# Block products for w_down, and one written list of steps: a transformer layer with linear attention and a bilinear GLU

## The chip, the cores and the metric

The kernel runs on one core of a Trainium2 chip. The metric is the device time of one execution in microseconds (us). Times before are the median of three runs; the profile is of one further execution. A core has TensorE (PE: matmuls, with PEld for weight loads), VectorE (DVE), ScalarE (ACT), GpSimd (POOL) and SyncE (SP), which here only issues transfers. Each works through its own queue in order.

## The reference

```python
xn = layernorm(x)                                  # x: 2048 tokens x 512, bf16
q, k, v = split(xn @ wqkv)                         # 32 heads of 16
phi(t) = concat(softmax(t @ w_phi), softmax(-(t @ w_phi)))   # 32 features a head
kv, z  = sum over tokens of phi(k) v and of phi(k)
attn   = (phi(q) kv) / (phi(q) z + 1e-6) @ wo
glu    = ((xn @ w_gate) * (xn @ w_up)) @ w_down    # hidden width 1792
out    = x + attn + glu
```

## The kernel before

The 2048 tokens are 16 tiles of 128; four tiles make a group (T is 0 to 3). The hidden width is 14 chunks of 128 columns. `wgu` holds w_gate and w_up, `wd` w_down, `wo` the output weights, all in SBUF for the whole run. The program is scheduled by hand: each engine runs its instructions in the order in which the Python code issues them.

1. Start (to about 12 us): the first four tiles are centred and transposed on TensorE, and v is computed for them.
2. Groups 0 and 1, with the k side: `half` makes a gate or an up chunk for 512 tokens with four matmuls of 512 columns, `gate_copy` takes the gate to SBUF on ScalarE, `hidden` multiplies on VectorE into `hT`. In between come `fold` (w_phi folded into the k and q weights), v and k of each tile, and `features`: two exponentials on ScalarE, a reduction (L300) and a reciprocal (L302) on VectorE, and the feature product on GpSimd (L304). `kv` sums phi(k) v into two PSUM tiles. The load of the transposed q weights is issued on SP (L659) behind the first four transposes of normalized tiles and ahead of the next eight.
3. `attend(n)` divides and makes `otok`, which SP's queue transposes to `oT`. `fin(n)` is one output tile: 14 matmuls of `hT` with `wd` and 4 of `oT` with `wo`, all into one bank of 512 columns; VectorE adds x, and SP sends the tile out (L387, L398, L399).
4. Groups 2 and 3: gate and up are computed by seven block products instead of eight. `pair_block(k, g)` takes 1024 tokens as two row blocks, the 512 inputs as two inner blocks, and the chunks k and k + 7 as two column blocks. It needs sums of tokens (`ss`, L454), sums of weights (`T`, L445, four for each k, half of them on VectorE), and products p1 to p7 that ScalarE keeps (L493, L495) and VectorE joins (L499, L503). For the up half, GpSimd multiplies by the gate (L504). Output tiles 4 to 7 fill the gaps between the products.
5. From about 181 us: output tiles 9 to 15, with the last q tiles and `attend` one tile ahead. The last tile is cut at 384 columns, so that the last bank has 128 columns.

w_gate and w_up are scaled by powers of two, one for each pair of chunks (`weight_norm`, `weight_up`). PSUM is eight banks: six in rotation (`bank`) and two for the pool of the phase (v, kv, attention, or `fin`).

Of the kernel before, what the change touches and what calls it, by code (L numbers as in the profile page):

```python
# [15 lines left out]
PSUM = bass.MemoryType.PSUM  # L16


def _bcast_ap(ap_in: bass.AP, new_ap):
    return bass.AP(tensor=ap_in.tensor, offset=ap_in.offset, ap=new_ap)  # L20


@with_exitstack
def kernel(
# [40 lines left out]
    consts = ctx.enter_context(tc.tile_pool(name="consts", bufs=1))  # L65
    wpool = ctx.enter_context(tc.tile_pool(name="wpool", bufs=1))
# [7 lines left out]
    wgu = wpool.tile([P, 2, DC, F], BF16)  # L74
# [60 lines left out]
    xnT = xpool.tile([P, DC, HALF], BF16)  # L135
# [11 lines left out]
    for i in range(NV):  # L147
        vt = vpool.tile([P, 8, 4, E1], BF16, name=f"vt{i}", tag="vt")
        nc.vector.memset(vt[:, :, :, DH:E1], 1.0)
        vts.append(vt)  # L150
# [9 lines left out]
    def bank(name, dt=F32, n=TT):  # L160
        return ps_s.tile([P, n], dt, name=name, tag="s")
# [26 lines left out]
    def subtract(n, *means):  # L188
        xns[n] = xnpool.tile([P, D], BF16, name="xn", tag="x")
# [12 lines left out]
    def centre_by_halves(n):  # L202
        h = D // 2
        part = consts.tile([P, 2], F32)
        junk = xnpool.tile([P, 2, h], BF16, name="junk", tag="x")
# [5 lines left out]

    chores = []

    def chore(k=1):
        for _ in range(min(k, len(chores))):
            chores.pop(0)()

    def ln_block(lo):
        mv = mv_tile()
        nb = lnpool.tile([P, GT], F32, name="nb", bufs=GT)  # L220
        rstd = []

        def scales():
            r = lnpool.tile([P, GT], F32, name="rstd", bufs=GT)
            ln_rstd(mv, GT, r[:])
            nm = lnpool.tile([P, GT], F32, name="nm")
            nc.gpsimd.tensor_scalar(out=nm[:], in0=mv[:, :, 0], scalar1=-1.0, scalar2=None, op0=ALU.mult)
            nc.gpsimd.tensor_tensor(out=nb[:], in0=nm[:], in1=r[:], op=ALU.mult)
            rstd.append(r)

        def apply(i):
            late = lo + i >= QT
            xn = xnpool.tile([P, D], F16 if late else BF16, name="xn", tag="x")
            if late:
                nc.gpsimd.tensor_scalar(out=xn[:], in0=xall[:, lo + i, :], scalar1=rstd[0][:, i:i + 1],
                                        scalar2=nb[:, i:i + 1], op0=ALU.mult, op1=ALU.add)
            else:
                nc.scalar.activation(out=xn[:], in_=xall[:, lo + i, :], func=AF.Identity,
                                     scale=rstd[0][:, i:i + 1], bias=nb[:, i:i + 1])
            nc.sync.dma_start(out=xt(lo + i), in_=xn[:], transpose=True)  # L240

        for i in range(GT):
            chores.append(lambda i=i: ln_stats(lo + i, mv[:, i, :]))
        chores.append(scales)
        for i in range(GT):
            chores.append(lambda i=i: apply(i))
# [18 lines left out]
    def fold(qk, dst, j0):  # L265
        R = P // 2
        banks = [bank("pq").rearrange("p (j c x) -> p j c x", j=2, c=DC) for r in range(2)]
        for j in range(2):
            for c in range(DC):
                for r in range(2):  # L270
                    rows = slice(r * R, (r + 1) * R)
                    nc.tensor.matmul(banks[r][:, j, c, :], lhsT=wT2[rows, qk, c, (j0 + j) * P:(j0 + j + 1) * P],  # L272
                                     rhs=bd[rows, c, 4 * r:4 * r + 4, :].rearrange("p a b -> p (a b)"),
                                     start=True, stop=True)
        dv = dst[:, j0:j0 + 2, :].rearrange("p j (c r x) -> p r j c x", c=DC, r=2)
        nc.scalar.copy(out=dv[:, 0], in_=banks[0])
        nc.vector.tensor_copy(out=dv[:, 1], in_=banks[1])

    def fold_both(qk, dst):
        for j0 in (0, 2):  # L280
            fold(qk, dst, j0)
# [6 lines left out]
    def features(n, w, name, pf=None):  # L288
        if pf is None:
            pf = bank(name)  # L290
            proj(pf, n, w)
        e = epool.tile([P, NG, 2, 4 * DH], F32, name="e")
        pfv = pf.rearrange("p (g c) -> p g c", g=NG)
        nc.scalar.activation(out=e[:, :, 0, :], in_=pfv, func=AF.Exp,  # L294
                             scale=rst[:, n:n + 1] if n < GT else 1.0)
        nc.scalar.activation(out=e[:, :, 1, :], in_=pfv, func=AF.Exp,  # L296
                             scale=nrst[:, n:n + 1] if n < GT else -1.0)
        ev = e[:].rearrange("p g s (h f) -> p (g s h) f", f=DH)
        sums = epool.tile([P, 2 * H], F32, name="sums")
        nc.vector.tensor_reduce(out=sums[:], in_=ev, axis=AX.X, op=ALU.add)  # L300
        rs = epool.tile([P, 2 * H, 1], F32, name="rs")
        nc.vector.reciprocal(out=rs[:].rearrange("p a b -> p (a b)"), in_=sums[:])  # L302
        phi = epool.tile([P, NG, P], BF16, name=f"phi{name}", tag="phi", bufs=4)
        nc.gpsimd.tensor_tensor(out=phi[:].rearrange("p g (x f) -> p (g x) f", f=DH), in0=ev,  # L304
                                in1=rs[:].to_broadcast((P, 2 * H, DH)), op=ALU.mult)
        return phi

    sends = []

    def qproj(n, held=False, new_bank=bank):  # L310
        q_begin(n, new_bank)
        q_end(held)

    q_open = []

    def q_begin(n, new_bank):
        pf = new_bank("q")
        proj(pf, n, W1q, lower)
        q_open.append((n, pf))

    def q_end(held=False):
        q_rest()
        q_features(held)

    def q_rest():
        n, pf = q_open[0]
        proj(pf, n, W1q, upper)

    def q_features(held=False):
        n, pf = q_open.pop()  # L330
        phiq = features(n, W1q, "q", pf)

        def send():
            phiqTs[n] = qtpool.tile([P, NG, P], BF16, name="phiqT")
            nc.sync.dma_start(out=phiqTs[n][:], in_=phiq[:].rearrange("p g c -> p (g c)"), transpose=True)

        sends.append(send)
        if not held:
            qsend()

    def qsend():
        sends.pop(0)()

    hTs = {}
    units = [(T, f) for T in range(NGRP // 2) for f in range(FC)]
# [8 lines left out]
    def gate_copy(ps, n):  # L354
        g_sb = gpool.tile([P, TT], BF16, name="g_sb")
        nc.scalar.copy(out=g_sb[:, 0:n], in_=ps)  # L356
        return g_sb

    def hidden(T, f, ps, g_sb, lo, hi):
        if T not in hTs:  # L360
            hTs[T] = hpool.tile([P, FC, TT], BF16, name="hT", tag="h")
        nc.vector.tensor_tensor(out=hTs[T][:, f, lo:hi], in0=ps, in1=g_sb[:, 0:hi - lo], op=ALU.mult)  # L362

    def unit(T, f, lo=0, hi=TT):
        pg = half(wg, "g", T, f, lo, hi)
        pu = half(wu, "u", T, f, lo, hi)
        hidden(T, f, pu, gate_copy(pg, hi - lo), lo, hi)

    def ffn(k):
        for _ in range(k):  # L370
            if units:
                unit(*units.pop(0))

    def fin_parts(n, new_bank, lo=0, hi=D):
        T, t4 = n // GT, n % GT
        w = hi - lo
        held = []

        rows = [(hTs[T][:, f, t4 * P:(t4 + 1) * P], wd[:, f, lo:lo + w]) for f in range(FC)]
        rows += [(oTs[n][:, c, :], wo[:, c, lo:lo + w]) for c in range(DC)]  # L380
        if n == 2 * GT:
            rows = [row for f, row in enumerate(rows) if f % FH != FH - 1 or f >= FC] + [rows[FH - 1], rows[FC - 1]]

        def mm(i):
            if i == 0:
                held.append(new_bank("fin")[:, 0:w])
            nc.tensor.matmul(held[0], lhsT=rows[i][0], rhs=rows[i][1], start=(i == 0), stop=(i == len(rows) - 1))  # L387
            if i == len(rows) - 1:
                store(held[0])

        def store(ps):
            o_sb = opool.tile([P, w], BF16, name=f"o_sb{w}", bufs=3 if w == D else 1)
# [10 lines left out]
    def fin(n, cuts=(0, D)):  # L403
        for lo, hi in zip(cuts, cuts[1:]):
            for part in fin_parts(n, bank, lo, hi):
                part()
# [374 lines left out]
    with tc.tile_pool(name="ps_ab2", bufs=1, space=PSUM) as ps_ab:  # L781
# [11 lines left out]
        for n in range(9, NT):  # L793
# [5 lines left out]
            if sends:  # L799
                qsend()  # L800
# [33 lines left out]
```

## Time and profile before

| | |
|---|---|
| median of three runs | 215.61 us (215.32 to 215.88) |
| the profiled execution | 215.67 us, span 213.9 us |
| granted TensorE clock | 1.00 |
| busy, share of the span | TensorE 98%, weight loads 48%, VectorE 76%, ScalarE 58%, GpSimd 60% |

The span runs from the first to the last instruction; the profiled execution's own time holds 1.8 us more. Matmuls are pipelined, so a row's mean duration of 379 ns is not what a matmul costs in a stream: their starts are. The same holds on the other engines to a smaller degree.

### The profile page before, as it was taken

The numbers are of one execution on the slowest core, as the hardware profiler recorded it, in microseconds if no ns is written. First come the engines' busy times: TensorE is split into PE (matmuls) and PEld (weight loads), VectorE is DVE, ScalarE is ACT, GpSimd is POOL, SyncE is SP. The second block draws the span as 40 slices with busy tenths as digits, with TensorE's granted clock in tenths as the row PEclk, the third lists the DMA queues.
The fourth block names the chain that finished last, engine by engine and source line by source line (L and its number), as shares of the span: only waits on it lengthen the run. The fifth ranks groups of instructions, "written<-read, shape, count | busy, mean of one in ns | idle before, by whom it ended". The sixth has DMA issues, their size and how long they took to land.

```text
span 213.9 us, 3610 instructions
## 1 busy us (share of the span) xinstructions
PE 210.1 (98%) x1280; PEld 101.7 (48%) x1280; DVE 163.2 (76%) x279; ACT 125.0 (58%) x219; POOL 129.2 (60%) x112
## 2 busy tenths in 40 slices
PE   8999999999999999999999999999999999999994
PEld 3664445444444444554444444444444444444543
DVE  5757979869867788887777897988969689776341
ACT  4635578998896999442666686868746352220000
POOL 3600557597895788859899497979788620333000
PEclk9999999999999999999999999999999999999999
DMA  5999995613022023234444202021120201333511
GB/s 152 266 281 385 374 287 87 91 26 75 0 51 52 0 49 81 66 40 112 100 101 100 49 0 52 0 74 25 48 49 3 74 26 34 91 98 98 126 49 49
DMA packets 47249, 19.91 MB, mean 93 GB/s; under 512 B 37504, under 2 KB 46976, under 8 KB 47104
## 3 DMA queue, kind: packets, MB, share of 16 engines
q1 hardware_dynamic: 47232, 19.69, 36.6%
q8 instruction: 10, 0.16, 0.3%
q14 instruction: 7, 0.06, 0.1%
HBM read 8.67 MB, written 2.10 MB: 50 GB/s over the span
## 4 chain that ended last, share of the span: by engine, by line
PE 98%; ACT 1%; DVE 0%; issue 0%
PE fin L387 29%; PE g L350 11%; PE u L350 11%; PE sa L487 11%; PE pv L285 7%; PE q L285 6%; PE k L285 6%; PE sc L487 6%; PE sb L487 3%; PE kv L622 2%; PE ab L686 2%; PE warm L554 2%; PE pq L272 1%; PE tp L253 1%; ACT k L493 0%; ACT xnT L256 0%
## 5 line engine op out<-in xcount | busy, mean ns | idle before, releaser
L387 PE MATMUL fin<-wd,hT 128*128 128x512 bf16 (+2 forms) x238 | 54.1, 366 | 0.0
L304 POOL TENSOR_TENSOR phiq<-e,rs 128x1024 bf16<-128x1024 f32 x16 | 30.9, 1934 | 25.6 <-DVE rs L302 18.1
L304 POOL TENSOR_TENSOR phik<-e,rs 128x1024 bf16<-128x1024 f32 x16 | 30.9, 1933 | 24.2 <-DVE rs L302 17.3
L300 DVE TENSOR_REDUCE sums<-e 128x64 f32<-128x1024 f32 x32 | 38.7, 1208 | 9.0 <-ACT e L296 9.0
L350 PEld LDWEIGHTS <-wgu 128*128 128x128 bf16 x240 | 23.1, 98 | 24.2
L387 PEld LDWEIGHTS <-hT 128*128 128x128 bf16 x238 | 22.3, 98 | 24.4
L350 PE MATMUL u<-xnT,wgu 128*128 128x512 bf16 (+1 forms) x120 | 29.1, 365 | 0.0
L350 PE MATMUL g<-xnT,wgu 128*128 128x512 bf16 (+1 forms) x120 | 28.9, 365 | 0.0
L504 POOL TENSOR_TENSOR hT<-u_sb,hT 128x512 bf16<-128x512 bf16 x18 | 21.1, 1185 | 10.1 <-DVE u_sb L503 10.1
L362 DVE TENSOR_TENSOR hT<-u,g_sb 128x512 bf16<-128x512 f32 (+1 forms) x30 | 18.6, 622 | 4.5 <-PE u L350 3.9
L356 ACT CAST g_sb<-g 128x512 bf16<-128x512 f32 (+1 forms) x30 | 17.1, 569 | 8.1 <-PE g L350 7.9
L294 ACT ACTIVATE e<-q 128x512 f32<-128x512 f32 x12 | 7.2, 598 | 23.6 <-PE q L285 23.6
L302 DVE RECIPROCAL rs<-sums 128x64 f32<-128x64 f32 x32 | 17.7, 552 | 2.5
L493 ACT ACTIVATE k<-sa,both 128x512 f32<-128x512 f32 x21 | 14.5, 688 | 8.7 <-PE sa L487 8.6
L495 ACT COPY k<-sa 128x512 f32<-128x512 f32 x21 | 12.3, 587 | 11.2 <-DVE u_sb L503 7.4
L398 DVE TENSOR_TENSOR o_sb<-fin,xall 128x512 bf16<-128x512 f32 (+2 forms) x13 | 8.4, 646 | 12.0 <-PE fin L387 12.0
L445 POOL TENSOR_TENSOR T<-wgu,T 128x512 f16<-128x512 bf16 x14 | 17.0, 1216 | 0.5
L387 PE MATMUL fin<-wo,oT 128*128 128x512 bf16 (+2 forms) x68 | 17.1, 366 | 0.0
L487 PEld LDWEIGHTS <-T 128*128 128x128 f16 x112 | 10.8, 98 | 13.1 <-issue 0.6
L487 PE MATMUL sa<-ss,T 128*128 128x512 f16 x56 | 16.7, 379 | 0.1
L435 ACT ACTIVATE wgu<-wgu,up 128x1024 bf16<-128x1024 bf16 x14 | 15.9, 1156 | 0.1
L420 ACT ACTIVATE junk<-wgu 128x1024 bf16<-128x1024 bf16 x14 | 15.1, 1083 | 0.0
(98 smaller groups left out, 352.1 us busy)
## 6 DMA issues: line engine op xcount, KB each, us to landing
out_dram<-o_sb SPq DMA_DIRECT2D x15, 128.0 KB, 1.9
wd<-in_B_w_down_dram SPq DMA_DIRECT2D x1, 1792.0 KB, 15.4
wgu<-in_B_w_gate_dram SPq DMA_DIRECT2D x2, 640.0 KB, 6.8
wgu<-in_B_w_up_dram SPq DMA_DIRECT2D x2, 640.0 KB, 8.0
xall<-in_A_x_dram SPq DMA_DIRECT2D x1, 1024.0 KB, 12.1
xall<-in_A_x_dram SPq DMA_DIRECT2D x4, 128.0 KB, 2.7
vk<-in_A_wqkv_dram SPq DMA_DIRECT2D x2, 256.0 KB, 3.6
wgu<-in_B_w_gate_dram SPq DMA_DIRECT2D x2, 256.0 KB, 4.9
```

The costliest lines, as they stand in the source:

```text
L285: nc.tensor.matmul(ps, lhsT=xt(n)[:, j, :], rhs=w[:, j, :], start=(j == 0), stop=(j == DC - 1))
L300: nc.vector.tensor_reduce(out=sums[:], in_=ev, axis=AX.X, op=ALU.add)
L302: nc.vector.reciprocal(out=rs[:].rearrange("p a b -> p (a b)"), in_=sums[:])
L304: nc.gpsimd.tensor_tensor(out=phi[:].rearrange("p g (x f) -> p (g x) f", f=DH), in0=ev, in1=rs[:].to_broadcast((P, 2 * H, DH)), op=ALU.mult)
L350: nc.tensor.matmul(ps, lhsT=w[:, c, f * P:(f + 1) * P], rhs=xnT[:, c, T * TT + lo:T * TT + hi], start=(c == 0), stop=(c == DC - 1))
L356: nc.scalar.copy(out=g_sb[:, 0:n], in_=ps)
L362: nc.vector.tensor_tensor(out=hTs[T][:, f, lo:hi], in0=ps, in1=g_sb[:, 0:hi - lo], op=ALU.mult)
L387: nc.tensor.matmul(held[0], lhsT=rows[i][0], rhs=rows[i][1], start=(i == 0), stop=(i == len(rows) - 1))
L435: nc.scalar.activation(out=cols, in_=cols, func=AF.Identity, scale=up2[:, k, g:g + 1])
L445: (nc.gpsimd if i % 2 or k < 2 else nc.vector).tensor_tensor(out=t[:, i], in0=a, in1=b, op=ALU.subtract)
L487: nc.tensor.matmul(held[name], lhsT=w[:, j, :], rhs=x[:, j, :], start=start and j == 0, stop=(j == hc - 1), skip_group_check=True)
L504: (nc.vector if k == FH - 1 else nc.gpsimd).tensor_tensor(out=dst, in0=u[:], in1=dst, op=ALU.mult)
```

## The change

The emission order becomes data. Each piece of work is a named step; a list of 1072 words, `ORDER`, says in which order they are issued, and a suffix /v, /g or /a says on which of VectorE, GpSimd and ScalarE. `SLOTS` names the buffer of each rotating tile. Steps in the list: g, u, gc, h (gate, up, gate copy, multiply of a chunk); vk, vc, kx, ky, kr, ki, kp, kv (k and v of a tile: products, copy, two exponentials, reduction, reciprocal, feature product, sum), and q alike; s, sc, a, xt (normalization and transpose of a tile); wq (load of the q weights); ab, de, rd, ot, oT (attention of a tile); f, fs, fo (products, store and transfer of an output tile); up, t, z, p, k, j, m, d (block products of gate and up).

What is new in the work:

- Output tiles 9, 10, 11 and 13, 14, 15 are computed in three pairs (n, n + 4) by seven block products each: the two tiles are two row blocks, the halves of the hidden width two inner blocks of 7 chunks, and two halves of 256 output columns. One product is 7 matmuls of 256 columns. `hT` of groups 2 and 3 is float16.
- S: four sums of hidden blocks for each of 7 chunks, 28 instructions of 128x384, into the memory of `wgu`. cb, ct: scaled float16 copies of w_down's quarters (12, on ScalarE), wt: its differences (8). They lie in the memory of `xnT`, of an `hT` and of the first tiles of x.
- K, A, B, J: keeps of a product in SBUF, adds, and joins into the output tile.
- One scale for each of w_gate, w_up and w_down, by a sum of squares (21 passes on ScalarE instead of 14).
- Some gate copies, v copies, m, t, S and keeps are on VectorE, others on GpSimd or ScalarE, as the list says.
- Turns: a GpSimd instruction that follows in the list a VectorE step with both inputs in SBUF waits for its end.
- The load of the q weights (wq) stands on SP's queue behind five transposes of normalized tiles.
- Tile 12 is the last of the full-width ones, cut at 384 columns; the pair (11, 15) is the last work.

```diff
+ORDER = """
+g2 gc2/v u0 g3 gc3/a u2 h2 g1 u1 gc1/v h1 fk2 g0 gc0/v u3 fka2/a h3 h0 fk0 fkv0/v g8 g4 fkv2/a fka0/a k0 gc8/v
...
+h5 kp1/g a8/g xt9 g15 g20 kv0 h14 wq n0.4 u20 g18 gc15/a n1.2 n0.6 gc18/a gc20/a s13 kr3 s12 s15 kr2 u18 vk5.0
...
+p4.0 fs2 p5.1 p5.0 j7.1 j7.0 rd4 ot4 wp2 t12/g d4.0/a p1.2 q6.0 q6.1 p4.1 p3.1 k1.2/a t22/g t20/g t21/g qx6 qy6
...
+j7.13 d4.13 rd13 fo5 ot13 qt15 m7.13/v S1.4/g S0.6/g S1.5/g S1.3/g m2.13/v f8.5 ab8 f12.8 p3.13 qy11 qx11
+cb22.1/a de8/v rd8 ot8 f12.6 P1a.10 f12.5 S1.0/v F12.4 F12.6 f12.3 F12.7 f8.0 F12.0 ab9 j3.13 S1.6/g S2.4/g
...
+P1a.9 P6a.10 rd9 ot9 fs12 qr11 Fs12 S2.3/v ct3.0/a f8.3 ab14 cb21.1/a K1.9/a ct3.1/a wt3.1/v P5a.10 P5b.10 P6a.9
...
+J2.10 X10 P4w.11 P4b.11 J4.11 X15
+"""
...
+    down_sub("t1", "t1", "b11")
+    down_sub("t2", "t2", "t1")
+    down_sub("t3", "b22", "t3")
+    down_sub("t4", "b21", "t2")
...
+    def hidden_sum(i, k, eng):
+        tok = slice(t0 * P, TT)
+        S = [wgu16[:, j // 2, t0:GT, ((j % 2) * FH + k) * P:((j % 2) * FH + k + 1) * P] for j in range(4)]
...
+        a, b, op = ((A21, A22, ALU.add), (S[0], A11, ALU.subtract), (A11, A21, ALU.subtract), (A12, S[1], ALU.subtract))[i]
+        eng.tensor_tensor(out=S[i], in0=a, in1=b, op=op)
...
+        product(1, "a", a(2, 0), d("b11"), True)
+        keep("k1", 1, "a")
+        add("k1", "A1", lambda: x(n, 0))
+        product(2, "b", a(2, FH), B21, True, (n, 0))
+        join(2, n, 0, "b", lambda: kept("k1"))
+        product(5, "d", s(0), d("t1"), True)
...
+        product(6, "a", s(1), d("t2"))
...
+        product(3, "c", s(3), d("b22"), True, (n, 1))
...
+        product(7, "a", s(2), d("t3"))
...
+        product(4, "a", a(3, FH), d("t4"), False, (m, 0))
+        join(4, m, 0, "a", lambda: x(m, 0))
...
+    both_in_sbuf = re.compile(r"(N?z|t|wt|c[bt]|S|N?m|[AB]|a|ws)\d")
+    turn = pool_last = None
+    for word in ORDER.split():
+        name, _, eng = word.partition("/")
+        fn, default = steps.pop(name)
...
+        if on_pool and turn is not None:
+            tc.add_manual_dep(on_pool[0], turn.name, AFTER, reason="turns")
+            turn = None
+        if on_dve and both_in_sbuf.match(name):
+            turn = on_dve[-1]
...
```

More of the change, by code (lines that the diff above doesn't have):

```diff
@@ L1 @@
+import re
 from contextlib import ExitStack
@@ L286, in proj, with hT @@
                              start=(j == 0), stop=(j == DC - 1))
[L288 to L342, printed above, removed]
+    V, G, A = nc.vector, nc.gpsimd, nc.scalar
     hTs = {}
-    units = [(T, f) for T in range(NGRP // 2) for f in range(FC)]
+    def hT(T):
+        if T not in hTs:
+            hTs[T] = hpool.tile([P, FC, TT], F16 if T >= NGRP // 2 else BF16, name="hT", tag="h")
+        return hTs[T]
     def half(w, name, T, f, lo, hi):
@@ L357, in gate_copy @@
+    def gate_copy(ps, n, eng=A):
+        g_sb = ring(gpool, "g", [P, TT], BF16, "g_sb")
+        copy(eng, g_sb[:, 0:n], ps)
         return g_sb
     def hidden(T, f, ps, g_sb, lo, hi):
[L360 to L392, printed above, removed]
-            xres = xall[:, n, lo:lo + w]
-            if n < GT:
-                nc.vector.scalar_tensor_tensor(out=o_sb[:], in0=ps, scalar=r2[:, n:n + 1], in1=xres,
-                                               op0=ALU.mult, op1=ALU.add)
-            else:
-                nc.vector.tensor_tensor(out=o_sb[:], in0=ps, in1=xres, op=ALU.add)
-            nc.sync.dma_start(out=out_view(n, n + 1)[:, 0, lo:lo + w], in_=o_sb[:])
-        return [lambda i=i: mm(i) for i in range(FC + DC)]
@@ L403, in fin @@
[L403 to L406, printed above, removed]
-    nrm = consts.tile([P, FH, 2], BF16)
-    up2 = consts.tile([P, FH, 2], F32)
-    down2 = consts.tile([P, FH, 2], F32)
-    both = consts.tile([P, FH], F32)
-    Ts = {}
-    def pair_cols(k):
-        return wgu[:].rearrange("p g c (h f) -> p g c h f", h=2)[:, :, :, :, k * P:(k + 1) * P]
-    def weight_norm(k, g):
-        junk = xnpool.tile([P, DC, 2, P], BF16, name="junk", tag="x")
-        with nc.allow_low_precision(reason="a bound for a power of two"):
-            nc.scalar.activation(out=junk[:], in_=pair_cols(k)[:, g], func=AF.Abs, accum_out=nrm[:, k, g:g + 1])
@@ L542 @@
-    norms = [(k, g) for k in range(FH) for g in range(2)]
-    def norm(k):
-        for _ in range(k):
-            if norms:
-                weight_norm(*norms.pop(0))
+        V.tensor_tensor(out=hT(T)[:, f, lo:hi], in0=ps, in1=g_sb[:, 0:hi - lo], op=ALU.mult)
     warm = bank("warm")
@@ new lines, with step, add, unit_steps @@
+    inv2 = consts.tile([P, 2], F32)
+    eps1 = consts.tile([P, 1], F32)
+    nc.gpsimd.memset(eps1[:], 1e-6)
+    steps = {}
+    held = {}
+    def step(name, default=None):
+        def add(fn):
+            steps[name] = (fn, default)
+        return add
+    def unit_steps(u):
+        T, f = u // FC, u % FC
+        lo = 2 * P if u < 2 else 0
+        @step(f"g{u}")
+        def _():
+            held["g", u] = half(wg, "g", T, f, lo, TT)
+        @step(f"gc{u}", A)
+        def _(eng):
+            held["gc", u] = gate_copy(held.pop(("g", u)), TT - lo, eng)
+        @step(f"u{u}")
+        def _():
+            held["u", u] = half(wu, "u", T, f, lo, TT)
+        @step(f"h{u}")
+        def _():
+            hidden(T, f, held.pop(("u", u)), held.pop(("gc", u)), lo, TT)
@@ new lines, with fold_steps, _ @@
+    for u in range(2 * FC):
+        unit_steps(u)
+    def fold_steps(name, qk, dst, j0):
+        R = P // 2
+        dv = dst[:, j0:j0 + 2, :].rearrange("p j (c r x) -> p r j c x", c=DC, r=2)
+        @step(f"f{name}{j0}")
+        def _():
+            banks = [bank("pq").rearrange("p (j c x) -> p j c x", j=2, c=DC) for r in range(2)]
+            for j in range(2):
+                for c in range(DC):
+                    for r in range(2):
+                        rows = slice(r * R, (r + 1) * R)
+                        nc.tensor.matmul(banks[r][:, j, c, :],
+                                         lhsT=wT2[rows, qk, c, (j0 + j) * P:(j0 + j + 1) * P],
+                                         rhs=bd[rows, c, 4 * r:4 * r + 4, :].rearrange("p a b -> p (a b)"),
+                                         start=True, stop=True)
+            held["f" + name, j0] = banks
+        @step(f"f{name}a{j0}", A)
+        def _(eng):
+            copy(eng, dv[:, 0], held["f" + name, j0][0])
+        @step(f"f{name}v{j0}", V)
+        def _(eng):
+            copy(eng, dv[:, 1], held["f" + name, j0][1])
@@ new lines, in vk_steps, with _, part @@
+    def vk_steps(n):
+        if n < GT:
+            @step(f"k{n}")
+            def _():
+                held["k", n] = bank("k")
+                proj(held["k", n], n, W1k)
+        else:
+            def part(js):
+                if js[0] == 0:
+                    held["v", n], held["k", n] = bank("pv"), bank("k")
+                for j in js:
+                    proj(held["v", n], n, wv, (j,))
+                    proj(held["k", n], n, W1k, (j,))
+            steps[f"vk{n}.0"] = (lambda: part((0, 1)), None)
+            steps[f"vk{n}.1"] = (lambda: part((2, 3)), None)
+            @step(f"vc{n}", A)
+            def _(eng):
+                copy(eng, vts[n % NV][:, :, :, 0:DH], held.pop(("v", n)).rearrange("p (a b c) -> p a b c", a=8, b=4))
+        feature_steps("k", n)
+        @step(f"kv{n}")
+        def _():
+            vt, phik = vts[n % NV], phis.pop(("k", n))
@@ new lines, with q_steps, part, _ @@
+    for b in range(2):
+        steps[f"kvm{b}"] = (lambda b=b: kv_scale(b), None)
+    def q_steps(n):
+        new_bank = bank_f if n in QF else bank
+        def part(js):
+            if js[0] == 0:
+                held["q", n] = new_bank("q")
+            proj(held["q", n], n, W1q, js)
+        steps[f"q{n}.0"] = (lambda: part((0, 1)), None)
+        steps[f"q{n}.1"] = (lambda: part((2, 3)), None)
+        feature_steps("q", n)
+        @step(f"qt{n}")
+        def _():
+            phiqTs[n] = ring(qtpool, "qt", [P, NG, P], BF16, "phiqT")
+            nc.sync.dma_start(out=phiqTs[n][:], in_=phis.pop(("q", n))[:].rearrange("p g c -> p (g c)"), transpose=True)
@@ new lines, in fin_steps, with part, _ @@
+    def fin_steps(n, tag="f", lo=0, hi=D):
+        T, t4, w = n // GT, n % GT, hi - lo
+        new_bank = bank_f if GT <= n < QT else bank
+        hrow = lambda f: (hT(T)[:, f, t4 * P:(t4 + 1) * P], wd[:, f, lo:hi])
+        orow = lambda c: (oTs[n][:, c, :], wo[:, c, lo:hi])
+        pairs = [(2 * i, 2 * i + 1) for i in range(FH)] if n < QT else [(k, k + FH) for k in range(FH)]
+        groups = [(hrow, p) for p in pairs] + [(orow, (0, 1)), (orow, (2, 3))]
+        done = []
+        def part(i):
+            if not done:
+                held["fin", n, lo] = new_bank("fin")[:, 0:w]
+            row, which = groups[i]
+            for c in which:
+                l, r = row(c)
+                done.append(c)
+                nc.tensor.matmul(held["fin", n, lo], lhsT=l, rhs=r, start=len(done) == 1, stop=len(done) == FC + DC)
+        for i in range(len(groups)):
+            steps[f"{tag}{n}.{i}"] = (lambda i=i: part(i), None)
+        @step(f"{tag}s{n}")
+        def _():
+            o_sb = held["o", n, lo] = (ring(opool, "o", [P, D], BF16, "o_sb") if w == D else opool.tile([P, w], BF16, name=f"o_sb{w}", bufs=1))
+            xres, ps = xall[:, n, lo:hi], held.pop(("fin", n, lo))
+            if n < GT or n >= QT:
+                V.scalar_tensor_tensor(out=o_sb[:], in0=ps, scalar=r2[:, n:n + 1] if n < GT else scale_of(n)[0],
+                                       in1=xres, op0=ALU.mult, op1=ALU.add)
+            else:
+                V.tensor_tensor(out=o_sb[:], in0=ps, in1=xres, op=ALU.add)
+        @step(f"{tag}o{n}")
+        def _():
+            nc.sync.dma_start(out=out_view(n, n + 1)[:, 0, lo:hi], in_=held.pop(("o", n, lo))[:])
@@ new lines, with scale_steps, _ @@
+    for g in range(3):
+        for k in range(FH):
+            steps[f"n{g}.{k}"] = (lambda k=k, g=g: weight_norm(k, g), None)
+    def scale_steps(lo, hi):
+        n = hi - lo
+        f, u = fro[:, lo:hi], up3[:, lo:hi]
+        @step(f"wr{lo}")
+        def _():
+            held["nrm", lo] = bank("nrm")[:, 0:n * FH]
+            nc.tensor.matmul(held["nrm", lo], lhsT=ones[:, 0:P], rhs=nrm[:, lo:hi, :].rearrange("p g k -> p (g k)"),
+                             start=True, stop=True)
+        @step(f"wf{lo}")
+        def _():
+            V.tensor_reduce(out=f, in_=held.pop(("nrm", lo)).rearrange("p (g k) -> p g k", g=n), axis=AX.X, op=ALU.add)
+        @step(f"wp{lo}")
+        def _():
+            G.tensor_scalar(out=f, in0=f, scalar1=2.0 ** -60, scalar2=None, op0=ALU.max)
+            G.tensor_tensor(out=u, in0=f, in1=mhalf[:, 0:n], op=ALU.pow)
+        @step(f"ws{lo}")
+        def _():
+            V.tensor_scalar(out=u.bitcast(I32), in0=u.bitcast(I32), scalar1=0x7F800000, scalar2=None, op0=ALU.bitwise_and)
+            V.tensor_scalar(out=u, in0=u, scalar1=levels[lo], scalar2=None, op0=ALU.mult)
+            V.reciprocal(out=down3[:, lo:hi], in_=u)
@@ new lines, in down_copy, with run, down_sub @@
+    def down_copy(name, quarter):
+        def run(eng, lo, hi):
+            copy(eng, down_tile(name)[:, lo:hi], quarters[quarter][:, lo:hi], up3[:, 2:3])
+        for i, (lo, hi) in enumerate(PIECES):
+            steps[f"c{name}.{i}"] = (lambda eng, lo=lo, hi=hi: run(eng, lo, hi), A)
+    def down_sub(name, a, b):
+        def run(eng, lo, hi):
+            eng.tensor_tensor(out=down_tile(name)[:, lo:hi], in0=down_tile(a)[:, lo:hi], in1=down_tile(b)[:, lo:hi],
+                              op=ALU.subtract)
+        for i, (lo, hi) in enumerate(PIECES):
+            steps[f"w{name}.{i}"] = (lambda eng, lo=lo, hi=hi: run(eng, lo, hi), V)
@@ new lines, with phase, run @@
+    dpool = ctx.enter_context(tc.tile_pool(name="dp", bufs=2))
+    kvps = []
+    def phase(name, bufs):
+        def run():
+            if pools:
+                stack.pop().close()
+                pools.clear()
+            new = ExitStack()
+            stack.append(new)
+            pools.append(new.enter_context(tc.tile_pool(name=name, bufs=bufs, space=PSUM)))
+            if name == "ps_k":
+                kvps.extend(pools[0].tile([P, 4, 4, E1], F32, name=f"kv{b}") for b in range(2))
+        return run, None
@@ new lines @@
+    stack = []
+    steps["=k"] = phase("ps_k", 1)
+    steps["=ab"] = phase("ps_ab", 1)
+    steps["=f"] = phase("ps_f", 2)
+    steps["=ab2"] = phase("ps_ab2", 1)
+    engines = dict(v=V, g=G, a=A)
+    both_in_sbuf = re.compile(r"(N?z|t|wt|c[bt]|S|N?m|[AB]|a|ws)\d")
[3 more added lines that the diff above has]
+        fn, default = steps.pop(name)
+        before = len(nc.cur_bb.bb.instructions)
+        if default is None:
+            fn()
+        else:
+            fn(engines[eng] if eng else default)
+        issued = nc.cur_bb.bb.instructions[before:]
+        on_pool = [i for i in issued if i.engine == ET.Pool]
+        on_dve = [i for i in issued if i.engine == ET.DVE]
+        if on_pool and turn is not None:
[3 more added lines that the diff above has]
+            turn = on_dve[-1]
+            if name.startswith("ws") and pool_last is not None:
+                tc.add_manual_dep(on_dve[0], pool_last.name, AFTER, reason="turns")
+        pool_last = on_pool[-1] if on_pool else pool_last
@@ L807 @@
+    assert not steps, sorted(steps)
+    stack.pop().close()
 _INS = ['A_x', 'A_wqkv', 'A_w_phi', 'A_wo', 'B_x', 'B_w_gate', 'B_w_up', 'B_w_down']
```

728 lines of the change are left out of this document (394 added, 334 removed).

## The prediction

> **What bounds the kernel now.** I read the page's part 1 and part 4 first, then the chain of waits in order of time for the last stretch, then busy time by window for the middle, then the timeline and the groups of the few instructions that the change multiplies.
>
> ```profile
> PE 210.1 (98%) x1280; PEld 101.7 (48%) x1280; DVE 163.2 (76%) x279; ACT 125.0 (58%) x219; POOL 129.2 (60%) x112
> PE 98%; ACT 1%; DVE 0%; issue 0%
> ```
>
> TensorE is busy for 98% of the span and makes 98% of the chain that ended last: no other engine's work is on the path, except in the first 7 us and after the last product.
>
> ```profile
> 11.89 0.44 PE g L350 x4
> 199.20 3.88 PE fin L387 x18
> 203.34 7.83 PE fin L387 x54
> 211.17 0.02 issue
> 211.19 0.29 DVE o_sb L398
> ```
>
> The chain prices a matmul as TensorE spaces it, not by its 379 ns from start to end. Eighteen of 512 columns take 3.88 us, so one costs 216 ns; four of 256 columns take 0.44 us, so one costs 109 ns. The last product ends at 211.17 us; 2.7 us follow (0.29 us of store, then the last transfer).
>
> ```profile
> 112.40:180.90 68.50, 68.41 (x351) 31.45 (x350) 57.87 (x90) 42.79 (x68) 48.03 (x38) 1.00 0.17 41
> ```
>
> This window is the stretch of the gate and up products by blocks. After length, its columns are TensorE, weight loads, VectorE, ScalarE, GpSimd, clock and DMA. TensorE stands still for 0.1 us in 68.5; VectorE is busy 84%, GpSimd 70%. Here the change adds the most.
>
> ```profile
> L445 DVE TENSOR_TENSOR T<-wgu x10: 414/894/1378, 122.8 to 161.2; 128x512 f16<-128x512 bf16 x10
> 150.15 0.69 DVE L510 TENSOR_TENSOR hT<-sa,hT 128x512 bf16<-128x512 f32 x1 [0.62 <-PE sa L487]
> 150.76 0.68 DVE L503 TENSOR_TENSOR u_sb<-sc,k 128x512 bf16<-128x512 f32 x1
> 151.36 1.71 DVE L445 TENSOR_TENSOR T<-wgu 128x512 f16<-128x512 bf16 x2
> 151.52 1.26 POOL L504 TENSOR_TENSOR hT<-u_sb,hT 128x512 bf16<-128x512 bf16 x1 [1.28 <-DVE u_sb L503]
> ```
>
> Two things are to be seen. VectorE starts its next instruction 0.61 us after one that is shown as 0.69: I call that distance the pitch and price by it. And a VectorE subtraction with both inputs in SBUF takes 414 ns, but 1378 when a GpSimd instruction (151.52) has started ahead of it. The mean of ten is 895 ns, so they were held 0.48 us each.
>
> **The change, part by part.**
>
> *w_down by seven products (six tiles in three pairs).* Removed per pair: 2 x 14 full-width products of hidden and w_down and 2 x 4 of oT and wo, 36 matmuls. Added per pair: 7 x 7 products of 256 columns and 4 x 4 for wo, 65 half-width ones. For three pairs: 108 x 216 ns = 23.33 us go, 195 x 109 ns = 21.26 us come. All of this lies on the path: **-2.07 us**. The Trainium skill, page "TensorE: Matmul & The Clock Gate", section "Back-to-back issue gap", gives a sustained spacing of about 81 ns for 128 columns and 131 ns for 512 when each matmul has its own weight load. By that rule a half-width matmul costs well over half of a full one (about 98 ns, an estimate on a line between its two figures), and the change would lose about 5 us. The rows of this kernel, each matmul with its own load, say 109 and 216, which is half; I go by them.
>
> *What the pairs need beside TensorE.* New: 28 sums of hidden halves (S, 128x384, two inputs in SBUF), 12 scaled copies of w_down and 8 subtractions for its sums, 12 keeps of half width, 12 adds, 12 joins instead of 6 stores, 7 more norms of weights (1.04 us pitch each on ScalarE). Pitches from the timeline: VectorE 0.34 us for a 512-wide sum in SBUF, 0.61 to 0.66 with PSUM, 1.24 for a reduction, 0.47 for its reciprocal; 0.27 for S and 0.39 for a half-width join are estimates from these by width; GpSimd 1.11 to 1.13 for 512, so about 0.88 for 384 (an estimate on the line to its 1024-wide 2.08), and 1.90 for a feature product. The list also moves 9 gate copies, 4 v copies and 11 multiplies m to VectorE.
>
> *The sum by stages.* Over the whole list VectorE gets 171 us by pitch, and with 5.5 us of the untouched start 176 of some 208 us. ScalarE gets about 132, GpSimd about 137. So TensorE stays the longest queue in total. The dense stretch goes from q6.0 to P5a.10 of the list: 72.4 us of products. VectorE there has 38 joins (23.6), 9 reductions (11.2), 8 reciprocals (3.8), 7 direct products (4.3), 7 otok (4.3) with 7 rden (2.7), 6 stores (3.8), 4 keeps (2.5), 13 m (4.4), 8 T (2.7), 6 S (1.6), 3 w_down subtractions (1.6) and 1.3 of small ones: 67.8 us, 94%. GpSimd has 15 S (13.2), 12 T (13.3), 8 feature products (15.2), 7 m (7.9), two subtractions (3.7) and 0.7: 54 us, 75%. VectorE has 4.6 us to spare. How much do the 31 of its steps with both inputs in SBUF lose to a running GpSimd instruction? Bounds: 0, if each comes when GpSimd stands still; 0.48 each as measured, 14.9 us, against which 4.6 us are free, so TensorE would stand still for 10 us. I take 0.1 each (3 us), nearer the lower end: the turns take away the case that the timeline above shows (a GpSimd instruction starting between two VectorE steps), and as VectorE is the fuller engine it is mostly GpSimd that arrives first at a turn and waits. Below nothing this term cannot go, since TensorE stood still for only 0.1 us here before.
>
> *Turns.* Each run of VectorE steps with both inputs in SBUF (50 steps in all) makes the next GpSimd instruction wait. Behind it GpSimd queues feature products, multiplies m and sums S. GpSimd's spare 18 us in the dense stretch hide that; if they are used up, the first to be late are the S sums ahead of P6a.10.
>
> *The written list.* It reorders gate, up, v, k and q products, each of unchanged width, so their sum stays. Gate columns 8 and 10 are used earlier: g8 at about 17.5 us and g10 at 21.8, by the sum of the products ahead. Of the packets of the four transfers that bring columns 4 to 13, half had ended by 17.1 us and three quarters by 19.8, so nothing, or a few tenths if a late packet is among them. Small waits for banks elsewhere in 200 us: 0 (as before) to 2 us; with the term above I take **+0.4 us** in all.
>
> *q weights behind the transposes.* SP's queue has this one transposing load after five transposes of xn instead of four. The fold that reads it stands at about 53 us and the load at about 40, against 5.5 us to landing: free, with 7 us of cover. Without the cover the fold's wait would be TensorE's.
>
> *The end.* The last product is now followed by a join of 256 columns (about 0.5 us: the 743 ns of 512 columns, less the 0.23 that the rows of L362 save at half width, 653 to 422) instead of 0.29, and its transfer is a full 128 KB (landing 1.9 us) instead of 32 KB (1.5), with another 128 KB just ahead. **+0.5 us**; bounds 0.2 and 0.9.
>
> Sum on the profiled execution: 213.9 - 2.07 + 0.4 + 0.5 = 212.7 us of span; 1.8 us lie around the span (215.67 against 213.9), so 214.5, and the median of the runs shown is 0.06 lower: **214.4 us**.
>
> **The rivals.**
>
> *A, forecast (0.56):* TensorE remains the bound with under 0.9 us of new stalls: 214.0 to 214.9.
>
> *B, the gain is eaten (0.13):* several tenths at banks whose reader on VectorE comes late, 1 to 2 us in all: 215.0 to 216.2. For it: VectorE's waits before were long (o_sb 12.0 us) and harmless because it had a quarter of its time free; in the dense stretch it has not. Against it: late-use work (reductions, otok) is most of what could slip.
>
> *C, VectorE becomes the bound of the dense stretch (0.24):* its SBUF steps still arrive in the middle of running GpSimd instructions. Price: 31 x 0.3 us = 9.3, less the 4.6 free, 4.7 us of TensorE standing still instead of 0.4: 218.7. It decides from about 0.15 us per step, where the free time ends, and makes the kernel slower than before from about 0.2. For it: the 1378 ns; a turn holds GpSimd back, but nothing holds VectorE back from starting into a running GpSimd instruction. The Trainium skill, page "SBUF — State Buffer", section "Who interferes with whom", says that the one that issues first has the shared pair for the whole instruction; the row agrees.
>
> *D, half-width products cost more than half (0.02):* at the 162 ns that the 384-column products before show (18 from 207.06 to 209.99 us), 195 of them would take 31.6 us instead of 23.3: 222.8. The 109 ns rows speak against it.
>
> *E, GpSimd late at the seam (0.05):* S1.3 stands behind m7.13's turn and three other S sums; 4 x 0.88 us from about 179.6 give 183.1, and P6a.10 needs it at 186.2. It decides beyond 3 us of delay; at 6 us TensorE loses 3: 217.0.
>
> **How the numbers follow.** About 0.3% (0.65 us) is what a measurement can tell from no change. Faster by more, below 214.96: A, 0.56. Within: B, 0.13. Slower: C, D and E, 0.31. Range: from 213.7 (A without stalls and the short end) to 217.8, which takes in B, E and the lower half of C; what is left out is the upper half of C, D and a little below.
>
> **What would show it.** Right: TensorE's busy time falls by about 2 us to 208, the half-width products stand 109 ns apart, it stays at 97 to 98% of chain and span, VectorE rises to about 180 us busy, T, m and S on VectorE stay near 0.3 to 0.5 us. Wrong: holes in TensorE between 115 and 190 us with VectorE or GpSimd as releaser (C if VectorE's S, m and T rows have maxima above 1 us, E if the hole stands at P6a.10), or a spacing well above 109 ns (D).

## The result, and the profile after

The changed kernel takes 214.84 us (median, 214.07 to 215.95) against 215.66 us (215.28 to 216.69) of the kernel before on the same chip: ratio 0.9965, interval 0.995 to 0.9979. Two later measurements of it gave 0.9958 (0.9943 to 0.9974) and 0.9967 (0.9948 to 0.9986). The profiled execution took 214.6 us, its span 212.8 (before: 215.67 and 213.9).

Parts 1 and 4 of the page after:

```profile
PE 207.8 (98%) x1368; PEld 109.8 (52%) x1368; DVE 181.5 (85%) x333; ACT 138.2 (65%) x247; POOL 140.3 (66%) x133
PE 91%; DMA 3%; DVE 2%; SPq 1%; issue 1%; DVEq 0%
```

TensorE is busy for 2.3 us less and is still 98% of the span; VectorE has gone from 163.2 to 181.5 us. The second line looks as if the path had moved to transfers and VectorE. It has not: the chain is followed back from its end, and on its way it meets one short wait of TensorE for a transpose and goes on behind that. Pieces of the chain of waits (start, length, what):

```profile
181.89 3.76 DMA oT<-otok
185.66 0.05 issue
185.70 0.60 PE fin L663 x2
...
196.65 2.08 PE da L924 x19
...
202.91 0.33 PE db L924 x3
...
208.48 0.78 PE da L924 x7
209.26 0.02 issue
209.28 0.48 DVE o_sb L953
```

Nineteen half-width products take 2.08 us, three take 0.33: 109 ns each. The product of tile 8's oT stands at 185.70 behind a transpose that landed 0.05 us before; the hole ahead of it is 0.22 us, and it is the only one of TensorE from 12 us to the last product.

Busy time from 115 to 190 us, first of the kernel before, then of the changed one (length; TensorE, weight loads, VectorE, ScalarE, GpSimd; clock, DMA):

```profile
115.00:190.00 75.00, 75.00 (x382) 34.52 (x382) 62.63 (x99) 43.31 (x69) 48.34 (x38) 1.00 0.18 45
```

```profile
115.00:190.00 75.00, 74.95 (x438) 37.47 (x437) 72.16 (x129) 47.80 (x82) 57.78 (x51) 1.00 0.31 60
```

VectorE is shown busy for 72.16 of 75 us, 9.5 more than before, and TensorE has lost nothing by it. Groups of the changed kernel by line, VectorE's steps with both inputs in SBUF (duration in ns: shortest, median, longest):

```profile
L819 DVE TENSOR_TENSOR hT<-u_sb,hT x14: 360/416/2186, 112.5 to 184.3; 128x512 f16<-128x512 bf16 x14
L758 DVE TENSOR_TENSOR T<-wgu x5: 413/417/801, 73.8 to 172.9; 128x512 f16<-128x512 bf16 x5
L758 DVE TENSOR_TENSOR T<-wgu,T x5: 411/419/1039, 106.6 to 165.5; 128x512 f16<-128x512 bf16 x5
```

The medians are those of a step that nobody holds; one step was held for 1.8 us (2186 ns). Over the 48 such steps the time above the undisturbed duration adds up to 4.7 us, 0.1 us each; 3.7 us of it lie in these 75 us, where the prediction put 3.

### The profile page after: what moved, and what is told of

Read it like the earlier page. It is cut to its first block, busy times and chain, and to the rows that moved or that the text cites. A ratio compares the mean times of both kernels' runs of the same rounds, so it can differ in the third digit from the quotient of the medians.

```text
span 212.8 us, 3868 instructions
## 1 busy us (share of the span) xinstructions
PE 207.8 (98%) x1368; PEld 109.8 (52%) x1368; DVE 181.5 (85%) x333; ACT 138.2 (65%) x247; POOL 140.3 (66%) x133
## 4 chain that ended last, share of the span: by engine, by line
PE 91%; DMA 3%; DVE 2%; SPq 1%; issue 1%; DVEq 0%
PE fin L663 16%; PE g L333 12%; PE u L333 11%; PE sa L797 11%; PE k L319 6%; PE pv L319 6%; PE q L319 6%; PE sc L797 5%; PE da L924 4%; PE sb L797 3%; PE kv L574 2%; DMA oT<-otok 2%; PE db L924 2%; PE dd L924 2%; PE dc L924 2%; PE ab L611 2%
## 5 line engine op out<-in xcount | busy, mean ns | idle before, releaser
L663 PE MATMUL fin<-wd,hT 128*128 128x512 bf16 (+2 forms) x154 | 37.9, 360 | 0.0
L663 PEld LDWEIGHTS <-hT 128*128 128x128 bf16 (+1 forms) x154 | 14.5, 98 | 14.8
L262 POOL TENSOR_SCALAR ve<-mv 128x1 f32<-128x1 f32 (+1 forms) x7 | 2.1, 293 | 24.9 <-DVE mv L258 24.8
L521 ACT ACTIVATE e<-k 128x512 f32<-128x512 f32 x24 | 13.3, 598 | 6.8 <-PE k L319 6.7
L521 ACT ACTIVATE e<-q 128x512 f32<-128x512 f32 x24 | 13.5, 601 | 6.4 <-PE q L319 6.3
L797 PEld LDWEIGHTS <-T 128*128 128x128 f16 x112 | 10.6, 98 | 11.9
L339 ACT CAST g_sb<-g 128x512 bf16<-128x512 f32 (+1 forms) x21 | 11.4, 568 | 7.1 <-PE g L333 6.5
L341 ACT ACTIVATE k<-sa 128x512 f32<-128x512 f32 x19 | 11.3, 602 | 6.1 <-PE sa L797 6.1
L319 PEld LDWEIGHTS <-xnT 128*128 128x128 bf16 x96 | 9.0, 98 | 10.7 <-ACT xnT L307 1.4
L758 POOL TENSOR_TENSOR T<-wgu,T 128x512 f16<-128x512 bf16 x9 | 10.6, 1176 | 5.8 <-DVE T L758 3.9
L319 PEld LDWEIGHTS <-x 128*128 128x128 f16 x96 | 9.0, 98 | 10.1 <-DVE otok L639 0.2
```

Source lines behind the costliest of these rows:

```text
L319: nc.tensor.matmul(ps, lhsT=xt(n)[:, j, :], rhs=w[:, j, :], start=(j == 0), stop=(j == DC - 1))
L339: A.copy(out=dst, in_=src)
L521: A.activation(out=held[s + "e", n][:, :, sign, :], in_=held[s, n].rearrange("p (g c) -> p g c", g=NG), func=AF.Exp, scale=(nrst if sign e ...
L663: nc.tensor.matmul(held["fin", n, lo], lhsT=l, rhs=r, start=len(done) == 1, stop=len(done) == FC + DC)
L797: nc.tensor.matmul(mine[bankname], lhsT=ww[:, j, :], rhs=xx[:, j, :], start=start and j == 0, stop=(j == hc - 1), skip_group_check=True)
```

## The experiments

**The same kernel again**, for its scatter.

> The changed kernel once more, as the yardstick of the kernels sent with it, and for a second profile. Theory 'columns' (TensorE is still the bound; 2.07 us of columns gone, about 0.9 us of it given back after the last product): 214.8 us, last product near 209.5 us, at most 0.5 us of holes between TensorE's products after the first 12 us. Rival 'VectorE is already the bound in some executions' (the 20 executions spread from 214.07 to 215.95 us, the kernel before mostly from 215.3 to 216.0): a profile slower than the first by some tenths shows them as holes between 115 and 190 us, with VectorE behind them.

214.83 us, ratio 0.9958. Its span was 213.8 us, 1.0 longer than in the first profile, with 4.3 us held on VectorE in the same places. The difference lies at the two ends and at tile 8: TensorE waited 0.72 us at 7.5 us for data, and 0.57 us at 186.5 us, a little more than the 0.5 us expected, where this line of the chain stands in place of the 3.76 us above:

```profile
182.39 4.11 DMA oT<-otok
```

So the rival, scatter by VectorE's holds, fell.

**Without the turns.** The dependencies that make GpSimd wait are left out, and with them the one that makes VectorE wait for GpSimd ahead of its `ws` steps (its line is changed in the same way).

```diff
-        if on_pool and turn is not None:
+        if False and on_pool and turn is not None:
```

> The waits that the list adds as turns are left out; data still orders everything. The first profile shows VectorE's steps with both inputs in SBUF held by 4.7 us in all, 0.09 us each. If the turns are what keeps this low: holds rise to 0.2 to 0.3 us each, 10 to 15 us, more than VectorE has free in the dense stretch, TensorE gets holes of 0 to 4 us, and the time is 215.8 us (215.2 to 218). If the order in the list alone keeps it low: holds stay near 5 us and the time stays within 0.3 us of the changed kernel.

221.48 us, ratio 1.0284 (1.0246 to 1.0323): 6.65 us more than the changed kernel, where I had expected about 1 us (215.8) and 218 us at the most. The groups of its lines:

```profile
L819 DVE TENSOR_TENSOR hT<-u_sb,hT x14: 361/726/2149, 113.6 to 192.4; 128x512 f16<-128x512 bf16 x14
L758 DVE TENSOR_TENSOR T<-wgu x5: 407/415/2150, 74.1 to 180.9; 128x512 f16<-128x512 bf16 x5
```

The median of L819 has gone from 416 to 726 ns, and 22 of the 48 steps were held, 16.8 us in all (0.35 each). The timeline shows how (start, length, engine):

```profile
153.03 1.16 POOL L758 TENSOR_TENSOR T<-wgu 128x512 f16<-128x512 bf16 x1
153.12 1.35 DVE L758 TENSOR_TENSOR T<-wgu,T 128x512 f16<-128x512 bf16 x1
153.12 1.08 ACT L521 ACTIVATE e<-q 128x512 f32<-128x512 f32 x2 [0.76 <-POOL phiq L543]
154.15 2.12 POOL L543 TENSOR_TENSOR phiq<-e,rs 128x1024 bf16<-128x1024 f32 x1
154.39 2.15 DVE L758 TENSOR_TENSOR T<-wgu 128x512 f16<-128x512 bf16 x1
```

A step of 0.41 us that starts behind a GpSimd instruction lasts until that one has ended, and two in a row put the join behind them 3 us late. The Trainium skill, page "SBUF — State Buffer", section "Who interferes with whom", says that the second to issue is blocked until the first has finished; the two VectorE rows agree with it (they end at 154.47 and 156.54, their GpSimd partners at 154.19 and 156.27). TensorE then stood still for 2.6 us until 159.4, and the windows of this kernel show a second price:

```profile
155.00:160.40 5.40, 2.89 (x13) 1.26 (x13) 5.37 (x7) 1.09 (x2) 4.64 (x5) 1.00 0.31 70
160.40:164.00 3.60, 3.60 (x10) 1.27 (x9) 2.89 (x4) 0.96 (x2) 0.86 (x1) 0.53 0.00 0
```

After TensorE had been busy for 2.89 of 5.40 us, its granted clock over the next 3.60 us was 0.53, which is 3.4 us at half speed: another 1.7 us. The chain shows it, during the fall and behind it:

```profile
161.89 1.71 PE sa L797 x4
164.24 0.43 PE q L319 x2
```

Matmuls of 512 columns stand 428 ns apart there, and 215 ns again from 164 us. The holes (0.8 at 103, 0.7 at 116, 1.7 at 147, 2.6 at 159) and this make 7.5 us of the 7.8 by which this execution (222.62 us) is longer than the changed kernel. The median of 221.48 us holds no such fall: the mean clock is 0.992 in the profiled execution and in the slowest (224.04 us), but 0.999 or 1.000 in the other four, which took 220.85 to 221.49 us. No trace of one of those four was kept, so where their holes stand is not shown.

**Full width in place of the pairs.** The six tiles as 14 + 4 matmuls of 512 columns, without S, cb, ct, wt and keeps; list, turns and the other moves stay.

```diff
-... S0.0/g S2.0/g ... cb11.1/a ... wt1.1/v ... P1a.10 ... P1b.9 ...
+... f14.0 ... f13.0 ...
```

> The same list, turns and engines, with the three pairs computed as six tiles of full width in their places; the sums S, the copies and differences of w_down and the joins of the pairs are left out. 'Columns': TensorE gets its 2.07 us back, and the last store is of 512 columns (0.65 us) instead of a join of 256 (0.48): 217.0 us (216.6 to 217.4), about 1.3 us above the kernel before. Rival 'VectorE bounds': VectorE is relieved of some 12 us after 115 us, so the time rises by clearly less than 2 us, to 215.2 to 216.2.

216.58 us, ratio 1.0041 (1.0027 to 1.0056), at the lower edge of what 'columns' expected: the block products are worth 1.75 us net, against 2.07 less what they cost elsewhere. Without them the list is 0.4% slower than the kernel before. By the two profiles all of that is its end: the last product starts at 210.91 us (210.94 in the kernel before), and 3.94 us follow instead of 2.99, with a store of 512 columns where the kernel before has one of 128 (0.29):

```profile
205.89 5.41 PE fin L658 x25
211.30 0.03 issue
211.33 0.75 DVE o_sb L668
```

**The last transfer in halves, first try.** The first half's transfer (Y15) stands in the list right behind the step that completes it, J8.11.

```diff
-... J8.11 P3a.10 ... oT11 fo12 P3b.9 ...
+... J8.11 Y15 P3a.10 ... oT11 fo12 P3b.9 ...
```

> The output of the last tile, 15, is sent as two halves of 256 columns, the first as soon as its join is done, about 4 us before the end; the last transfer is 64 KB instead of 128. If the size of the last transfer is part of the 0.9 us given back: landing falls from 1.73 to about 1.55 us, time 0.1 to 0.25 us lower than the changed kernel. If landing is a fixed cost: within 0.1 us of it.

216.02 us, ratio 1.0005 (0.9988 to 1.0021): 1.2 us lost. SP's own timeline, and the chain:

```profile
205.03 0.33 SPq L983 DMA_DIRECT2D out_dram<-o_sb  x1
205.45 1.19 SPq L646 DMA_TRANSPOSE oT<-otok  x1
```

```profile
205.45 2.42 DMA oT<-otok
207.87 0.05 issue
207.92 0.94 PE dc L925 x7
```

SP works through its queue in order. The new issue waited there for J8.11 until 205.03, and tile 11's transpose behind it went out at 205.45 instead of 203.15 (first profile) or 204.0 (second); TensorE had a hole of 1.31 us. The landing did fall, from 1.7 to 1.5 us. The mistake was mine, in the place and not in the idea.

**A dose of VectorE work: 3.7 and 7.4 us.**

```diff
+        steps[f"extra{i}"] = (lambda: V.tensor_reduce(
+            out=extra[:], in_=xall[:, 8:10, :].rearrange("p n (a f) -> p (n a) f", f=16), axis=AX.X, op=ALU.add), None)
-... p4.4 j7.3 k1.5/a ...
+... p4.4 j7.3 extra0 k1.5/a ...
```

> The changed kernel with three more VectorE reductions (128x1024 bf16 of the resident x into a tile that nothing reads, about 1.24 us each, 3.7 us in all) spread over the dense stretch. Theory (VectorE's free time between 115 and 190 us is the margin of this change, 75.0 less 72.2 shown busy, 2.8 us): part of the 3.7 us cannot be absorbed, TensorE gets 1 to 2 us of holes, about 216.0. Rival (much of VectorE's late-use work can slip past 190 us, where it is busy 14.9 of 22.8): within 0.4 us of the changed kernel, 214.8 to 215.2.

> The same with six more reductions, 7.4 us of VectorE in the dense stretch. Theory: 7.4 against 2.8 us free leaves 4.6 us of holes in TensorE, about 219.4, more if a hole is long enough for the granted clock to fall as it did without the turns. Rival (work slips): under 217.

216.65 us, ratio 1.0036 (1.0015 to 1.0056), and 217.48 us, ratio 1.0064 (1.0048 to 1.008). Against the changed kernel's 0.9963 (mean of its three ratios) that is +1.6 and +2.2 us. Busy time from 115 to 190 us, 3.7 us first:

```profile
115.00:190.00 75.00, 73.38 (x418) 36.25 (x423) 72.59 (x128) 47.27 (x80) 58.04 (x51) 1.00 0.30 59
```

```profile
115.00:190.00 75.00, 72.75 (x403) 35.23 (x409) 74.16 (x129) 46.38 (x78) 57.40 (x51) 1.00 0.30 59
190.00:215.60 25.60, 21.93 (x216) 18.87 (x215) 18.11 (x41) 5.80 (x14) 10.20 (x13) 0.98 0.39 83
```

Both profiles lack 21 records of matmuls; a profile of a kernel without these doses that lacks as many (the mended tail, below) shows 74.63 us of TensorE here. So TensorE loses 1.3 and 1.9 us in this stretch, most of the difference in time. The smaller dose is the theory's; the larger one costs half of what the theory said, and more than its rival (under 217 us). VectorE is at 99% there with 7.4 us, and what it does not get done it does later: 18.1 us after 190 us, where the changed kernel has 14.9. So there is no margin for work ahead of a join, and some for work that can slip.

**The same 7.4 us in the kernel before.**

> The kernel before with the same six reductions, one after the third step of each second pass of the first pair of groups' block products, where VectorE has 10.6 of 68.5 us free. Theory: absorbed, within 0.3 us of the kernel before (215.7); so the changed kernel has given away this margin. Rival: a reduction in front of a join costs a bank wait each time whatever the free time, 6 x 0.3 to 0.6 us, 217.5 to 219.

217.12 us, ratio 1.0044 (1.0028 to 1.0059): +0.9 us, though VectorE had 10.6 us free in the stretch. Neither the theory's number nor the rival's. The chain shows the same pieces three times; one of them:

```profile
152.26 1.63 DVE T L445 x2
153.89 1.13 DVE extra L728
155.02 0.67 DVE hT L499
155.69 0.04 issue
155.73 0.59 PE sc L487 x2
```

Behind two T the extra step makes the join (hT) late for its bank. In this profile the last product starts 1.3 us later than in that of the kernel before, about 0.2 us for each of the six steps. A free share of 15% does not cover a single step in the wrong place. The same dose costs 2.2 us in the changed kernel. Its six steps stand in other places there, so the 1.3 us between the two tests is not shown to be margin alone.

**The tail mended.** Y15 behind the transpose of tile 11 and the transfer of tile 12; and f8.7, the first two products of tile 8 with oT, exchanged with f8.4, two of its products with hT that stand later.

```diff
-... f8.1 f8.7 P1a.9 ... P5b.9 f8.4 qi11 ... oT11 fo12 P3b.9 ...
+... f8.1 f8.4 P1a.9 ... P5b.9 f8.7 qi11 ... oT11 fo12 Y15 P3b.9 ...
```

> The changed kernel with two moves: the last output tile's transfer in two halves of 256 columns, the first of them issued behind the transpose of tile 11 (not ahead of it as in the earlier run), and product f8.7 exchanged with the later f8.4, so that the final wo product of tile 8 does not meet a transpose that is still on its way. Theory: 0.22 to 0.57 us of TensorE's hole at 186 us and 0.15 us of the last transfer go: 214.2 to 214.5. Rival (f8.4 meets the same transpose, and the end is set by the last half alone): 214.8.

214.61 us, ratio 0.993 (0.9911 to 0.9948). It was measured again beside the changed kernel on one chip:

> The changed kernel once more, as the measure for the two others of this call: 0.9955 to 0.997 of the kernel before.

> The kernel of the run with the tail mended (f8.7 exchanged with f8.4, the last transfer in two halves, the first half's issue behind tile 11's transpose) once more, beside the changed kernel on one chip. Theory: 0.4 to 0.7 us below the changed kernel. Rival: the earlier difference was one between chips, and the two agree within 0.2 us.

214.26 us (214.0 to 214.51), ratio 0.9931 (0.992 to 0.9943), against 215.15 us (214.11 to 216.19), ratio 0.9967: 0.9 us less, the intervals apart, and the best version of this case; against the mean of the changed kernel's three ratios it is 0.7 us. The two moves were not measured apart, but each shows in the profile. There is no hole at tile 8 any more. And SP's wait for the last transfer, in the changed kernel measured beside it and then in the mended one (us in total, times, longest):

```profile
SPq L1071 <- DMA out_dram<-o_sb: 2.4, 1, 2.4
```

```profile
SPq L1076 <- DMA out_dram<-o_sb: 1.2, 1, 1.2
```

The full 128 KB took 2.8 us to land in this execution of the changed kernel, against 1.7 in the first two profiles; 64 KB took 1.5. Two profiles of the halves are too few to show that these never meet the longer landing; the narrower scatter of the times would fit it.

**The load of the q weights behind four transposes**, as in the kernel before.

```diff
-... xt5 h7 ... h14 wq n0.4 ...
+... xt5 wq h7 ... h14 n0.4 ...
```

> The changed kernel with the load of the q weights moved forward in the list, behind four transposes of normalized tiles as in the kernel before, instead of five. Theory (the fold that reads it is far behind its landing in both): the same time as the changed kernel within 0.2 us. Rival (the load holds up the transposes behind it on SP, or the fold waits): a hole of TensorE between 35 and 60 us moves, 0.3 us or more either way.

214.64 us, ratio 0.9953 (0.9937 to 0.9968), beside 0.9967 (0.9948 to 0.9986) of the changed kernel: within the intervals. The load is issued at 34.2 us instead of 42.4, lands after 4.7 instead of 4.4 us, and the fold reads it at 53 us in both. Its span is 212.8 us, that of the first profile, and its last product starts at the same time within 0.01 us. By the profile the placement is free; the times do not exclude some tenths.

## Why the prediction was right, step by step

The forecast was A, 214.4 us; 214.84 was measured, and 212.8 us of span where the sum said 212.7. The measured time lies near the upper edge of A (214.0 to 214.9). Two terms of the sum came out otherwise, the stalls smaller and the end longer, and partly cancelled.

- *Half-width products, -2.07.* Right: 109 ns each in the rows above, so case D (162 ns) falls. The Trainium skill, page "TensorE: Matmul & The Clock Gate", section "Back-to-back issue gap", would have about 98 ns for a half-width product (an estimate between its two figures) and 131 for a full one; the measurement, 109 and 216, decides against it here. The last product starts at 208.97 us instead of 210.94, 1.96 earlier; in the same list at full width it starts at 210.91, so the gain on TensorE is that of the pairs. D's own price was added up wrongly: 195 products at 162 ns are 10.3 us more than 195 at 109, so 224.7 us and not 222.8, outside the range all the same.
- *Stalls, +0.4.* 0.22 us, and not where I looked: no bank wait and no hole at the seam (rival E), but tile 8's transpose, which the sum did not list. The kernel before had a hole of 0.25 us at 114.9 us by the starts of its products, which the changed one has not, so against it the stalls are about nothing; "below nothing this term cannot go" read the busy time (0.1 us), which shows less. The written list puts f8.7 where that transpose, 3.8 to 4.1 us in the chain, is just landing.
- *Holds of 0.1 us for each VectorE step, and the turns.* Right in size (4.7 us over 48 steps) and in its reason: without the turns it is 0.35, which is rival C. Its price was too low. I had 4.7 us of standing still for C; the medians differ by 6.65 us. In the trace, 5.0 us of holes lie between 115 and 190 us, near the 4.7, and 0.8 us at 103, ahead of the stretch that C priced. The fall of the clock after a hole, 1.7 us more in that execution, the prediction did not consider.
- *VectorE at 94% of the dense stretch.* 96% by busy time, which counts each step a little longer than its pitch. The doses agree: 3.7 us more and TensorE stands still.
- *The end, +0.5.* Mis-sized, inside its bounds: from the start of the last product to the end of the span it is 3.84 us instead of 2.99. The join makes 0.24 of it (0.48 against 0.29 us, and a longer last matmul), near its price of 0.2, and the landing 0.25 (1.73 against 1.48), less than the 0.4 priced. The rest, 0.36 us, comes after the landing, in the semaphores that close the program, which I had taken as equal (1.29 against 0.93). Why they are longer is open: without the turns, and at full width, they take 1.0 us, in every other version of the changed list 1.29 to 1.46, so neither the list nor the pairs alone make it.
- *q weights, +0.* As said, with 6 us of cover instead of 7.
- *The columns g8 and g10.* A weight load waited 0.3 us for a gate column; TensorE's row has no hole there.

That the profiled execution lies 0.24 us below the median fits the scatter of the start, of one transpose and of the end: the three profiles of this kernel differ by the start (0.7 us), by tile 8's transpose (0.4) and by the last landing (1.1), not by VectorE.

## What to carry to other kernels

Before work is spread over VectorE and GpSimd, count VectorE's steps with both inputs in SBUF, and order the two engines there by a wait of the engine that has time; here that was worth eight times the gain of the change. A share of free time is no margin by itself: what counts is whether a step stands ahead of one that frees a bank, and a dose of harmless work shows it. An added issue on an in-order queue belongs behind every transfer that the longest queue waits for, even when its own data come earlier.

## What was not expected of the hardware

After the hole of 2.6 us (2.89 us busy in 5.40) the granted clock was halved for 3.4 us in the profiled execution without the turns; in four of that kernel's six executions the mean clock shows no such fall. The Trainium skill, page "TensorE: Matmul & The Clock Gate", section "Part 1: The HAM clock gate (the "warmup" mystery)", gives a window of 3413 ns in which activity is judged and an idle window as what lowers the clock. The length at half speed agrees with that window; a hole shorter than it was enough in this execution.
